# Loading the last 64 tokens of q and k with groups of tokens outermost instead of heads

## The chip, the core and the metric

One core of a Trainium2 chip runs the whole program. The metric is the device time of one execution in microseconds; the time of the kernel before is the median of three runs. A profile of one execution lies beside it.

## What is computed

Windowed attention over 8 batches, 8 heads, 576 tokens and 64 dimensions, followed by a dense two-layer block over all 4608 tokens. The first four heads see the last 32 tokens ("plain"), the other four every fourth of the last 128 ("dilated").

```python
scores = scale * np.matmul(q, k.transpose(0, 1, 3, 2))
mask_plain = (rel >= 0) & (rel < window)                                             # window = 32
mask_dil = (rel >= 0) & (rel < window * dilation) & (rel % dilation == 0)            # dilation = 4
...
attn = softmax(np.where(masks, scores, -1e9))
x = np.matmul(attn, v).transpose(0, 2, 1, 3).reshape(B * S, H * D)
h = x @ w_in                   # 512 -> 2048
g = np.maximum(0.01 * h, h)
out = g @ w_out                # 2048 -> 512
```

## The kernel before

All work is put into a plan first: each task has its engines, a duration by a cost model, the tasks that it depends on and a priority. The planner lists the tasks in a fixed order, and the program issues them so; on the chip each engine then works through its own instructions in that order and waits on semaphores. Nearly all DMAs are issued by SyncE (SP), so their order is fixed too. The change alters no task, no duration in the model and no priority, so each engine's instructions stand in the same order in both kernels.

The batches are worked in order. The first two (those below `EARLY`) are treated otherwise than the later six: their q, k and v are loaded in rows of 256 elements, four tokens of 64 dimensions, so that tokens with the same remainder by four end up together. 576 tokens are 144 such groups, and a tile has 128 partitions. So each early batch comes in two parts: part 0 has the first 128 groups, part 1 the remaining 16 groups, which are the last 64 tokens. Part 1 is loaded for all eight heads at once by `load_rest` (line 519): one load of q and one of k into a staging tile `stg` of 128 partitions, one partition for each pair of head and group, 256 elements of q and 256 of k in each; a load of v follows. GpSimd casts the staged rows to fp16 into the tile `rest` (by the helper at line 344, which records every cast).

In `turn` (line 654), with `part == 1`, TensorE turns `rest` in eight transposes (line 719) into the PSUM tile `tpb`. There the partitions are the 64 dimensions (twice), and the columns are numbered by o (0 for q, 1 for k), by the token's place in its group, and by the partition that the row had in `rest`. VectorE then copies (helper `move`, recorded at line 640) the columns of each head into the tiles `qbd` and `kt`, which the profile calls `slots`, at the places where the scores' matmuls want them. Where the slots of two heads' pairs are neighbours, one copy moves both; here that is so for every copy, 64 partitions by 128 elements each, eight copies for each early batch, in the order q, k for one half of the partitions and q, k for the other, the dilated heads ahead of the plain ones. Their order of columns differs: q of the dilated heads is written in runs of 16, k of the dilated heads to every fourth column; q of the plain heads in runs of 16, and k of the plain heads in runs of four tokens, read with a step of 128 columns.

Around this part in the program stand the casts of the weights w_in and w_out (line 344, on GpSimd, VectorE and, at line 342, ScalarE), the first dense layer (`up`, line 1069, with its activation at line 1080), the second (`down`, line 1240), the scores (lines 862 to 881) and the values of part 0 and 1 (lines 913 to 945), the normalisation (lines 957 to 963). In the first 60 us SP issues the q, k and v of the two early batches and all weights; the loads of `load_rest` are issued at 13.09 and 13.93 us for the first batch and at 41.26 and 45.06 us for the second, in the order of the plan's `FIRST`.

Of the kernel before, what the change touches and what calls it, by code (L numbers as in the profile page):

```python
# [211 lines left out]
def kernel(  # L212
# [14 lines left out]
    B, H, S, D = q.shape  # L227
# [7 lines left out]
    HS = S * D  # L235
# [16 lines left out]
    def bank(name, dt=FP32):  # L252
        return ps.tile([128, 512 if dt == FP32 else 1024], dt, name=name)

    def at(tl, p0, p1, off, *dims):

        row = tl.ap[0][0]
        return bass.AP(tensor=tl.tensor, offset=tl.offset + p0 * row + off,
                       ap=[[row, p1 - p0]] + [list(d) for d in dims])

    def dram(t, off, *dims):
        return bass.AP(tensor=t.tensor, offset=t.offset + off, ap=[list(d) for d in dims])
# [6 lines left out]
    PAD = 32  # L269
# [39 lines left out]
    tpb = bank("tp", FP16)  # L309
# [42 lines left out]
    def ring(name, n, users):  # L352

        r = rings.setdefault(name, [])
        waits = r[-n] if len(r) >= n else []
        r.append(users)
        return (len(r) - 1) % n, waits
# [24 lines left out]
    def clear_ones(slots, deps, prio=-700):  # L382
        for i in slots:
# [10 lines left out]
                   lambda e, h=h: ENG[e].memset(sides[64 * h:64 * h + 64, 64 * h:64 * h + 64], 1.0),  # L394
# [124 lines left out]
    def load_rest(b, prio):  # L519


        _, r_old = ring("REST", 1, r_users := [])
        sn, s_old = ring("STG", NST, s_users := [])
        st, lo = stg[sn], []
        for o, src in ((0, q), (1, k)):
            lo.append(load("SP", at(st, 0, 128, o * 256, [1, 256]),
                           dram(src, b * H * HS + 512 * D, [HS, 8], [4 * D, 16], [1, 256]),
                           128, 1024, s_old, prio))
        c = cast(at(rest, 0, 128, 0, [128, 8], [D, 2], [1, D]),
                 at(st, 0, 128, 0, [D, 8], [0, 2], [1, D]), 1024, lo + r_old, prio)  # L530
        s_users.append(c)
        vs, v_old, v_users = v_late[b]
        spread = bass.AP(tensor=vs.tensor, offset=vs.offset + 1024,
                         ap=[[4 * vs.ap[0][0], 16], [256, 4], [1, 256]])
        lv = load("SP", spread,
                  dram(v, (b * H + 4) * HS + 512 * D, [4 * D, 16], [HS, 4], [1, 256]),
                  64, 1024, v_old + [t_vr], prio)
        for vi in (2, 3, 0, 1):
            vt, d_users = kept[b, vi]
            c_v = []  # L540
            if vi >= 2:
                c_v = [cast(at(vt, 0, 64, 0, [1024, 2], [128, 4], [1, D]),
                            at(vs, 0, 64, 1024 + (vi - 2) * 256, [512, 2], [D, 4], [1, D]), 512,
                            [lv] + d_users, prio + 30)]
                v_users += c_v
            visits[b, vi, 1] = rest, [c], r_users, vt, c_v + seen_ones[b, vi], d_users
# [107 lines left out]
    def turn(b, hp, part, prio):  # L654
# [11 lines left out]
        if b >= EARLY:  # L666
            if tn not in s_clear:
                f = slots.bitcast(FP32)
                s_clear[tn] = [add((("POOL", 0.36), ("DVE", 0.34)), None, 0.2, old,
                                   lambda e, h=h: ENG[e].memset(  # L670
                                       at(f, 64 * h, 64 * h + 64, tn * S + 32 * (1 - h), [64, 9], [1, 32]),
                                       0.0), prio, 0.0, "set") for h in range(2)]
            qs = kb[:, PAD:PAD + S]
            for h in range(2):
                p0 = 64 * h
# [69 lines left out]
        if part == 1:  # L745
            if hp == 2:
                _, q_old = ring("TP", 1, q_users := [])
                tq = add("PE", 0.46, 0.25, c_qk + [t_id] + q_old, turn_in(tpb, na, 0, 8), prio, 0.2)
                n_users.append(tq)
                turned_rest[b] = tq, q_users  # L750
            tq, q_users = turned_rest[b]
            other = slot_of[b, hp ^ 1]
            two = 2 if abs(other[0] - tn) == 1 else 1
            if two == 2 and hp % 2:
                new = pair_moves[b, hp ^ 1]
            else:
                new, busy = [], users + other[1] * (two == 2)
                for hh in range(2):
                    h, p0 = 4 * (hp // 2) + hp % 2 + 2 * hh, 64 * hh
                    for o, bk in ((0, qb), (1, kb)):  # L760
                        x, dims = 512 * o + 16 * h, [[128, 4], [1, 16]]
                        if dil:
                            c, to = (0, [[144, 4], [4, 16]]) if o else (hh * S + 128, [[144, 4], [1, 16]])
                        elif o:
                            c, to, dims = PAD + 512, [[4, 16], [1, 4]], [[1, 16], [128, 4]]
                        else:
                            c, to = hh * S + 488, [[24, 4], [1, 16]]
                        step = PAD + S if o else 2 * S
                        new.append(move(at(bk, p0, p0 + 64, c, [step, two], *to),
                                        at(tpb, p0, p0 + 64, x, [16, two], *dims), 64 * two,  # L770
                                        [tq] + zq + zk + (busy if dil and o else []), prio))
                pair_moves[b, hp] = new
            q_users += new
            ev += new
        else:
            if b == 0 and not dil:
                if hp == 0:
                    _, q_old = ring("TP", 1, q_users := [])
                    both = []
                    for x in range(2):  # L780
                        n_x, c_x, u_x = visits[b, x, 0][:3]
                        both.append(add("PE", 0.23, 0.25, c_x[:1] + [t_id] + q_old,
                                        turn_in(tpb[:, 512 * x:512 * x + 512], n_x, 0), prio, 0.2))
                        u_x.append(both[-1])
                    two_q.append((both, q_users))
                tq, q_users = two_q[0]
                x = 512 * hp
                made = q_to((x, x), 0, 96, tq)
                q_users += made
            else:  # L790
                _, q_old = ring("TP", 1, q_users := [])
                tq = add("PE", 0.23, 0.25, c_qk[:1] + [t_id] + q_old, turn_in(tpb, na, 0), prio, 0.2)
                n_users.append(tq)
                for lo, hi in ((0, 128),) if dil else ((0, 120), (120, 128)):
                    q_users += q_to((lo, lo), lo, hi, [tq])
                made = q_users[:]
            if b == 0:
                _, k_old = ring("TPK", 1, k_users := [])
                kb_in, c_in, k_eng = tpk, 0, ("DVE", "ACT")
            else:  # L800
                k_old, k_users, kb_in, c_in, k_eng = q_old, [], tpb[:, 512:1024], 512, ("DVE",)
            if (b, hp) == (0, 1):
                k_eng = ("DVE",)
            tk = add("PE", 0.23, 0.25, [c_qk[1], t_id] + k_old, turn_in(kb_in, na, 512), prio, 0.2)
            n_users.append(tk)
            k_users += k_to(tpk if b == 0 else tpb, c_in, 0, 128, 0, 128,
                            [tk] if b == 0 else [tk, tq], k_eng)
            if b == 0:
                k_turned.extend(k_users)
            else:  # L810
                for t in q_users:
                    t.deps.append(tk)
                q_users += k_users
            ev += k_users if b else made + k_users
            if b:
                ev += q_users
            if b == 0 and hp == 1:
                later = []
                for hh in range(2):
                    p0 = 64 * hh  # L820
                    for i, n, c in ((96, 24, 384), (120, 8, 480)):
                        later.append(move(
                            at(qbd[tn - 1], p0, p0 + 64, hh * S + c, [2 * S, 2], [24, 4], [1, n]),
                            at(tpb, p0, p0 + 64, i, [512, 2], [128, 4], [1, n]), 8 * n,
                            tq + zq + t_zero[tn - 1][0], prio + 30))
                q_users += later
                for x in range(2):
                    t_x, u_x, e_x = (tn, users, ev) if x else slot_of[b, 0]
                    slot_of[b, x] = t_x, u_x, e_x + later
                return ev, users, qb, kb  # L830
# [734 lines left out]
    for t, u in zip(pe, pe[1:]):  # L1565
        if t.start > WARM:
            break
        x = t.start + t.dur + 0.1
# [45 lines left out]
```

## Time and profile before

| what | value |
|---|---|
| median of 3 runs | 307.77 us (305.67 to 308.3) |
| the profiled execution | 304.43 us, its span 302.6 us |
| granted TensorE clock | 0.994 in the mean |
| busy: PE, DVE, ACT, POOL | 290.3, 248.3, 214.2, 129.4 us |
| DMA | 47.64 MB, 157302 packets, mean 157 GB/s |
| copies of line 640 | 45, of which 16 are those of part 1 (64x128 elements) |

PE is TensorE's matmuls, PEld its weight loads, DVE VectorE, ACT ScalarE, POOL GpSimd, SP SyncE. "Busy" is time in which an engine has an instruction under way, without waiting. The chain that ended last is followed back from the last instruction, at each step to what released it. The DMA share is the mean over the core's 16 DMA engines; it can be a little over 1 since packets overlap. Lines like `POOL rest L344 <- DMA stg<-in_k_dram: 0.8, 2, 0.5` say who waited for whom: us in total, how often, the longest.

### The profile page before, as it was taken

Reading aid. Unit: us, or ns where it says so; the run is one execution under the profiler, and the core shown is the slowest. Engines: PE = TensorE matmul, PEld = TensorE weight load, DVE = VectorE, ACT = ScalarE, POOL = GpSimd, SP = SyncE. Lnnn points to the kernel's source line nnn. Section 1 sums busy time; section 2 is a strip of 40 time slices with the busy share of each in tenths; the row PEclk is TensorE's granted clock in tenths of the full one; section 3 lists DMA queues with packets and bytes.
Section 4 is the critical chain, followed back from the end, with each engine's and each line's share of the span. In section 5 each row is a group of like instructions: output and inputs, shape, how many; then the busy total and the mean of one; then the engine's idle time right before and its main releaser. Section 6 shows DMA issues by size and latency. Waiting matters only on the chain.

```text
span 302.6 us, 8081 instructions
## 1 busy us (share of the span) xinstructions
PE 290.3 (96%) x3027; PEld 230.2 (76%) x3027; DVE 248.3 (82%) x485; ACT 214.2 (71%) x523; POOL 129.4 (43%) x175
## 2 busy tenths in 40 slices
PE   5989979999999999999999999999999999999995
PEld 2635644657997788778877787778999999999984
DVE  5778897675999999998997997989998868577662
ACT  3799773696896885885867787466868877777511
POOL 5378776159828828835926656761000000000000
PEclk9999989999999999999999999999999999999999
DMA  7999998979889879658985988973102210031034
GB/s 247 334 339 404 397 363 174 185 149 209 157 173 199 147 152 218 121 131 146 189 156 137 165 173 167 162 191 101 42 2 77 64 37 1 2 107 35 2 111 132
DMA packets 157302, 47.64 MB, mean 157 GB/s; under 512 B 137296, under 2 KB 154576, under 8 KB 157264
## 3 DMA queue, kind: packets, MB, share of 16 engines
q1 hardware_dynamic: 156688, 46.79, 65.2%
q8 instruction: 23, 0.38, 0.5%
q10 hardware_dynamic: 576, 0.35, 0.4%
q14 instruction: 15, 0.12, 0.1%
HBM read 37.68 MB, written 9.44 MB: 156 GB/s over the span
## 4 chain that ended last, share of the span: by engine, by line
PE 62%; DVE 11%; ACT 7%; POOL 6%; DMA 5%; SPq 5%; issue 3%; POOLq 0%; ACTq 0%; DVEq 0%
PE fps L1331 16%; PE hps L1069 12%; PE hps L1153 7%; PE tp L1331 6%; SPq L333 5%; PE fps L1240 4%; PE ops L1153 3%; DMA stg<-in_q_dram 3%; PE ops L1012 2%; ACT gt L1080 2%; DVE ee L1022 2%; ACT w_in L342 2%; DVE turned L693 2%; PE sps L1153 2%; POOL slots L699 2%
## 5 line engine op out<-in xcount | busy, mean ns | idle before, releaser
L1069 PE MATMUL hps<-xt,w_in 128*128 128x384 f16 (+1 forms) x556 | 99.5, 307 | 0.8 <-DVE w_in L344 0.4
L1080 ACT ACTIVATE gt<-hps 128x384 f16<-128x384 f32 (+1 forms) x139 | 63.4, 460 | 26.2 <-PE hps L1069 25.1
L1331 PEld LDWEIGHTS <-gt 128*128 128x128 f16 x768 | 72.9, 98 | 9.6
L1069 PEld LDWEIGHTS <-w_in 128*128 128x128 f16 x576 | 49.1, 98 | 22.7 <-issue 1.2
L344 POOL CAST v_all<-vst 64x1152 f16<-64x1152 f32 (+3 forms) x36 | 41.1, 1150 | 15.6 <-DMA vst<-in_v_dram 14.1
L1331 PE MATMUL fps<-w_out,gt 128*128 128x256 f16 x368 | 47.5, 272 | 0.0
L344 POOL CAST nat<-stg 128x576 f16<-128x576 f32 (+1 forms) x49 | 34.5, 726 | 16.9 <-DMA stg<-in_q_dram 10.6
L1041 DVE TENSOR_TENSOR xt<-ops,rc 128x288 f16<-128x288 f32 x48 | 26.7, 557 | 5.3 <-PE ops L1012 2.6
L1022 DVE TENSOR_TENSOR ee<-ee,late_m 128x384 f16<-128x384 f16 (+1 forms) x48 | 25.4, 540 | 2.9 <-ACT ee L1019 2.8
L678 DVE STREAM_TRANSPOSE slots<-nat 64x64 f16<-64x64 f16 (+1 forms) x48 | 23.9, 497 | 0.5
L699 POOL COPY slots<-turned 64x512 f16<-64x512 f16 x24 | 19.0, 791 | 8.5 <-DVE turned L693 7.7
L1153 PEld LDWEIGHTS <-w_in 128*128 128x128 f16 x256 | 22.1, 98 | 0.5
L1033 ACT ACTIVATE rc<-rc 128x288 f32<-128x288 f32 x48 | 21.3, 449 | 0.5
L1360 ACT COPY stg<-fps 128x512 f32<-128x512 f32 (+1 forms) x24 | 12.8, 535 | 12.2 <-PE fps L1331 10.7
L693 DVE STREAM_TRANSPOSE turned<-nat 128x576 f16<-128x576 f16 (+1 forms) x24 | 17.6, 738 | 2.1 <-POOL nat L344 1.2
L706 POOL COPY slots<-turned 128x576 f16<-128x576 f16 x12 | 9.8, 819 | 20.7 <-DVE turned L693 20.4
L1240 PE MATMUL fps<-w_out,gt 128*128 128x512 f16 x64 | 16.9, 400 | 0.0
L1012 PEld LDWEIGHTS <-sides 128*128 128x128 f16 x240 | 14.0, 97 | 3.7 <-issue 0.8
L1153 PEld LDWEIGHTS <-stg 128*128 128x128 f16 x192 | 16.5, 98 | 0.3
L1163 ACT COPY rc<-hps 128x384 f32<-128x384 f32 x24 | 11.5, 479 | 7.4 <-PE hps L1153 5.5
L640 DVE COPY slots<-tp 64x128 f16<-64x128 f16 (+7 forms) x43 | 13.8, 334 | 3.5 <-PE tp L719 2.7
L1012 PE MATMUL ops<-ee,v_all 128*128 128x96 f16 (+2 forms) x240 | 16.4, 199 | 0.0
(145 smaller groups left out, 597.5 us busy)
## 6 DMA issues: line engine op xcount, KB each, us to landing
stg<-in_q_dram SPq DMA_DIRECT2D x48, 144.0 KB, 3.4
stg<-in_k_dram SPq DMA_DIRECT2D x48, 144.0 KB, 2.9
vst<-in_v_dram SPq DMA_DIRECT2D x12, 288.0 KB, 3.6
vst<-in_v_dram SPq DMA_DIRECT2D x24, 128.0 KB, 2.7
gt<-in_moe_w_in_dram SPq DMA_DIRECT2D x5, 512.0 KB, 7.8
xt<-in_moe_w_out_dram SPq DMA_DIRECT2D x3, 512.0 KB, 10.2
gt<-in_moe_w_out_dram SPq DMA_DIRECT2D x3, 512.0 KB, 9.5
vst<-in_v_dram SPq DMA_DIRECT2D x3, 384.0 KB, 10.2
```

The lines of the kernel that those rows point to most:

```text
L344: ENG[e].tensor_copy(out=dst, in_=src)
L678: nc.vector.transpose(at(qb, p0, p0 + 64, p0 + c, *dims), na[p0:p0 + 64, S + c // 2:S + c // 2 + n])
L693: lambda e, xb=xb, o=o, n=n: nc.vector.transpose(xb[:, 0:n], na[:, o * S:o * S + n]),
L699: lambda e, xb=xb, p0=64 * h: ENG[e].tensor_copy(out=at(qb, p0, p0 + 64, p0, [128, 4], [512, 2], [1, 64]), in_=at(xb, p0, p0 + 64, 0, [1, ...
L1012: nc.tensor.matmul(at(bk, 0, 128, o, *dims), stationary(s), et[:, c:c + n], start=i == 0, stop=i == len(parts) - 1, skip_group_check=True)
L1022: lambda e: nc.vector.tensor_tensor(out=et[:, 0:w], in0=et[:, 0:w], in1=mk, op=ALU.mult), prio + 0.1)
L1041: lambda e: nc.vector.tensor_tensor(out=dst, in0=at(ot, 0, 128, 0, *src), in1=at(rt, 0, 128, 0, *src), op=ALU.mult), prio + 0.2)
L1069: nc.tensor.matmul(ht[:, 0:n], at(w_in, 0, 128, i * DFF + j // 2 * 256 + j % 2, [2, 128]), at(xt[m % 2], 0, 128, i * 1152 + x0 + x, [1, n] ...
L1080: lambda e: nc.scalar.activation(out=gt[c % NG][:, j * n_c + x:j * n_c + x + n], in_=ht[:, 0:n], func=AF.Prelu, alpha=0.01),
L1153: nc.tensor.matmul(bk[:, 192 * jj:192 * jj + 192], w(i, 2 * jp + jj), x(i), start=first and jj == 0 and i == 0, stop=jj == 1 and i == 1, s ...
L1240: nc.tensor.matmul(ft, g[:, j * n_c + tt * 128:j * n_c + tt * 128 + 128], w_out[:, j * DM:j * DM + DM], start=(j == 0), stop=(j == NJ - 1))
L1331: nc.tensor.matmul(bk[:, x:x + HN], tl[:, off + j * step:off + j * step + 128], rhs(j), start=first and x == 0 and j == 0, stop=j == HJ - ...
```

## The change

In `load_rest` the two outer dimensions of the source are exchanged: 16 groups of tokens (step 4 x 64 elements) come first, then the 8 heads (step 576 x 64 elements). The destination is the same 128 partitions by 256 elements, so that partition p holds head p mod 8 and group p div 8, where before it held head p div 16 and group p mod 16. In `turn` the copies follow: the columns of one head start at h instead of 16 h, and lie eight apart instead of side by side; the two heads of one copy are 1 apart instead of 16.

```diff
         for o, src in ((0, q), (1, k)):
             lo.append(load("SP", at(st, 0, 128, o * 256, [1, 256]),
-                           dram(src, b * H * HS + 512 * D, [HS, 8], [4 * D, 16], [1, 256]),
+                           dram(src, b * H * HS + 512 * D, [4 * D, 16], [HS, 8], [1, 256]),
                            128, 1024, s_old, prio))
...
                     for o, bk in ((0, qb), (1, kb)):
-                        x, dims = 512 * o + 16 * h, [[128, 4], [1, 16]]
+                        x, dims = 512 * o + h, [[128, 4], [8, 16]]
                         if dil:
                             c, to = (0, [[144, 4], [4, 16]]) if o else (hh * S + 128, [[144, 4], [1, 16]])
                         elif o:
-                            c, to, dims = PAD + 512, [[4, 16], [1, 4]], [[1, 16], [128, 4]]
+                            c, to, dims = PAD + 512, [[4, 16], [1, 4]], [[8, 16], [128, 4]]
                         else:
                             c, to = hh * S + 488, [[24, 4], [1, 16]]
                         step = PAD + S if o else 2 * S
                         new.append(move(at(bk, p0, p0 + 64, c, [step, two], *to),
-                                        at(tpb, p0, p0 + 64, x, [16, two], *dims), 64 * two,
+                                        at(tpb, p0, p0 + 64, x, [1, two], *dims), 64 * two,
                                         [tq] + zq + zk + (busy if dil and o else []), prio))
```

The cast to `rest`, the transposes and the load of v are the same in both.

## The prediction

> **What bounds the kernel now.** I read the totals of the page first, then the stretches, the chain that ended last, the DMA issues, and at last the single instructions that the change touches. The totals and the granted clock:
>
> ```profile
> PE 290.3 (96%) x3027; PEld 230.2 (76%) x3027; DVE 248.3 (82%) x485; ACT 214.2 (71%) x523; POOL 129.4 (43%) x175
> ...
> PEclk9999989999999999999999999999999999999999
> ...
> PE 62%; DVE 11%; ACT 7%; POOL 6%; DMA 5%; SPq 5%; issue 3%; POOLq 0%; ACTq 0%; DVEq 0%
> ```
>
> The first line says that TensorE is busy nearly all the time, the last that it is 62% of the chain that ended last. The change touches only the first 56 us, so the question is what sets the pace there. The busy time by stretches (columns: us, PE, PEld, DVE, ACT, POOL, granted clock, DMA share, GB/s):
>
> ```profile
> 0.00:20.00 20.00, 15.47 (x129) 8.87 (x130) 13.06 (x41) 12.92 (x32) 10.00 (x25) 1.00 0.95 299
> 20.00:44.00 24.00, 20.76 (x183) 12.63 (x183) 20.78 (x56) 20.39 (x46) 19.77 (x32) 0.98 1.05 393
> 44.00:60.00 16.00, 16.00 (x125) 8.35 (x122) 11.96 (x29) 7.55 (x22) 7.02 (x10) 0.93 0.93 181
> ```
>
> From 20 to 44 us the DMA engines are full (share 1.05, 393 GB/s) and every engine is some 85% busy; from 44 us on TensorE has no idle time. So a delay of a load before 44 us can matter, and one behind it must reach TensorE to count. In the chain from 16 to 30 us stand ScalarE's casts of w_in and its activations, then TensorE's matmuls, from 37.7 to 42.5 us ScalarE, the normalisation and the `slots` copies on VectorE, then TensorE; the loads of `load_rest` and the cast to `rest` are nowhere in it. In the stretches of 4 us the granted clock is 0.87 from 40 to 44 and 0.70 from 44 to 48: a window of about 3.4 us at half speed, right behind the stretch in which TensorE was busy for 2.64 of 4 us. It costs 1.7 us. That is the largest single thing near the change.
>
> **The change, part by part.** *The loads.* For two batches `load_rest` issues one load of q and one of k (128 KB each) with 8 heads outermost; the change puts 16 groups of tokens outermost. Bytes, runs of 1 KB, issues and their order stay. What the old form does is seen in the DMA issues (size, then median us from issue to landing):
>
> ```profile
> vst<-in_v_dram SPq DMA_DIRECT2D x24, 128.0 KB, 2.7
> ...
> stg<-in_q_dram SPq DMA_DIRECT2D x2, 128.0 KB
> stg<-in_k_dram SPq DMA_DIRECT2D x2, 128.0 KB
> ...
> vst<-in_v_dram SPq DMA_DIRECT2D x2, 64.0 KB, 7.0
> ```
>
> A time to landing is given where each of the 16 DMA engines left its mark on the semaphore. Only the four loads of the change have none: the trace holds 28 marks fewer than 16 for each DMA, seven for each of them, which fits eight engines that carry the data and one mark for the eight that do not. The load of v beside them, whose outer count is 16 already, has all its marks. So I take it that the change spreads each load over 16 engines instead of 8. [...]
>
> The worth: at 393 GB/s over 16 engines 128 KB take 0.33 us, over 8 of them 0.67; a pair on 8 engines keeps these 0.67 us longer than needed. That is -0.67 us for each batch at the very most, -1.3 in all, if the loads behind set the pace; 0 if nobody waits. Who waits:
>
> ```profile
> POOL rest L344 <- DMA stg<-in_k_dram: 0.8, 2, 0.5
> ...
> PE hps L1069 <- DVE w_in L344: 0.4, 1, 0.4
> ...
> DVE w_in L344 <- DMA gt<-in_moe_w_in_dram: 0.4, 1, 0.4
> ```
>
> GpSimd's cast to `rest` waits 0.35 us in the first batch (21.65) and 0.49 in the second (48.57). In the first, GpSimd then casts v and w_in without a pause to 25.5 us, so 0.35 us can be passed to w_in; in the second the cast ends at 49.6 and its user, the eight transposes at line 719, comes at 53.4, so nothing is passed on. Of the loads behind, a w_in load makes VectorE wait 0.36 us at 23.2, and TensorE waits 0.43 us for a cast of VectorE at 28.8, but ScalarE, which stands in the chain from 16 to 30 us, waits there for no DMA. I take -0.2 us, nearer to the end of 0 because no DMA stands in the chain between 16 and 59 us. SP's issues behind the pair (w_in loads in the first batch; v, the late mask and batch 2 in the second) keep their order; the long issue at 41.26 (3.75 us) I read as a wait for room behind the 384 KB of v ahead of it, not for the pair.
>
> *The copies.* Sixteen copies of 64x128 elements (line 640) read the transposed tile in PSUM, eight a batch, two for q and two for k in each pair of heads. Single ones, in order q, k of the dilated heads, and k of the plain heads (ns):
>
> ```profile
> L640 DVE COPY slots<-tp x1: 215/215/215, 24.6 to 24.6; 64x128 f16<-64x128 f16 x1
> L640 DVE COPY slots<-tp x1: 438/438/438, 25.0 to 25.0; 64x128 f16<-64x128 f16 x1
> L640 DVE COPY slots<-tp x2: 216/244/271, 27.4 to 27.5; 64x128 f16<-64x128 f16 x2
> L640 DVE COPY slots<-tp x1: 283/283/283, 28.7 to 28.7; 64x128 f16<-64x128 f16 x1
> ```
>
> The q copies read and write runs of 16 neighbours: 215 ns. The plain k copies read every 128th element and write neighbours: 271 to 283. The dilated k copies read neighbours and write every fourth: 438. After the change a q copy reads every eighth element and writes neighbours; its nearest row is the plain k copy, so +60 ns, times eight, 0.48 us of VectorE in all, 0.24 a batch. A plain k copy reads every 128th element before and after, so 0. A dilated k copy already pays for its write; a strided read beside it is shown by no row. Bounds for that and for q: nothing at one end, +222 ns (438 less 216) at the other, for 12 copies 2.7 us. I take 0 for k. [...]
>
> On the path: in the first batch the copies stand between casts of w_in on VectorE (24.6 to 29.5), where TensorE waits 0.43 us for one such cast; of the 0.24 us I charge 0.1, since ScalarE's backlog there hides the rest (without that cover 0.24). VectorE's next idle moment is 0.54 us at 31.6, which ends the delay. In the second the eight copies (53.87 to 55.96) have their first user at 56.12, line 865, held by TensorE itself; the four dilated ones that it needs are done at 55.03, so 1.1 us cover the 0.12 added. Cost 0.
>
> *Sum.* -0.2 + 0.1 = -0.1 us on the profiled execution of 304.43 us (span 302.6 and 1.8 around it), so 304.3. The three runs shown lie higher: their median is 307.77, their mean 307.25. Less 0.1 that is 307.1 to 307.7; I say 307.4. The runs scatter by 2.6 us, so about 1% (3 us) is what a measurement of this kernel tells from no change.
>
> **The rivals.**
>
> *Faster: the front of the kernel is paced by DMA after all.* For it: GpSimd's casts follow the landings from 25 to 49 us (waits of 0.17, 0.25, 0.72, 0.54, 0.59, 2.11 and 0.49 us on DMA), and each engine fills its queue in program order. Then both 0.67 us come through, and if TensorE's stretch of 40 to 44 us closes up enough, the window at half clock goes too: -1.3 - 1.7 = -3.0, with the waits left over about -3.2: 304.5. Against it: the chain at 37.7 to 42.5 us is made of ScalarE, VectorE and TensorE. Chance 0.23.
>
> *Slower: the strided read holds VectorE, and TensorE falls idle into another window of half clock.* The place is 24.6 to 31 us, where the copies stand among the w_in casts. The price: up to 6 x 222 ns = 1.3 us of VectorE in the first batch, which its 0.54 us of idle time does not take up, so 0.8 us of idle TensorE, and a window like that at 43 us, 1.7 us, twice where the idle stretch straddles two: 0.8 + 3.4 = +4.2, 312.0; with one window +2.5. It passes 1% only with the second window or with a delay over 1.3 us. For it: TensorE is busy 3.35 of 4 us from 28 to 32 and 3.29 from 36 to 40, close to where the clock fell. Against it: PSUM reads with a far longer stride cost 60 ns. Chance 0.18.
>
> *The loads stay on eight engines.* Then only the copies' +0.1 is left, 307.9. The missing marks with an outer count of 8 and the full ones with 16 speak against it. Chance 0.04.
>
> **How the numbers follow.** No change that can be measured: 0.55 for my sum and 0.04 for loads that stay on eight engines, 0.59 within 1%. Faster by more 0.23, slower by more 0.18; both are larger than the sum alone suggests, because windows of half clock come in steps of 1.7 us and a program of fixed order shifts as a whole. The likeliest alone would be 305.6 to 309.0. The range reaches to the faster case and past one extra window: 303.9 to 310.2; left out are most of the slower rival and little on the other side.
>
> **What would show it.** In the profile after, the two 128 KB lines should carry a time to landing. GpSimd's wait for `stg<-in_k_dram` should fall below 0.8 us. The q copies should last about 275 ns, the dilated k copies 438, the plain ones 271 to 283; the sixteen together 0.5 us more. The window at half clock should still lie near 43 us. The prediction is wrong if copies of 64x128 take 450 ns or more, if the chain between 16 and 59 us has a DMA in it, or if windows of half clock come or go.

## The result

The changed kernel is slower: 309.57 us (median of 12 runs, 307.72 to 312.26) against 306.69 us for the kernel before on the same chip (12 runs, 304.47 to 310.95). The ratio is 1.0115, with a 95% interval of 1.0084 to 1.0147, some 3.5 us. The ratio leaves out the executions in a slower state, so it is not the quotient of the two medians (1.0094). The forecast was 307.4 us and no change that can be measured. The time lies in the range that was given, but by luck: the range reaches so far up for one more window of half clock, and none came. The case is the slower one, by none of the rivals' mechanisms.

The profiled execution of the changed kernel has a span of 308.7 us, 6.1 more than the one before. That overstates the difference, since the execution profiled before was faster than the fastest of its 12 runs here. The totals, the clock and the chain that ended last, from the page of the changed kernel:

```profile
PE 289.2 (94%) x3027; PEld 229.5 (74%) x3027; DVE 249.8 (81%) x485; ACT 214.6 (70%) x523; POOL 127.8 (41%) x175
...
PEclk9999999999999999999999999999999999999999
...
PE 56%; DMA 13%; DVE 12%; SPq 8%; POOL 5%; ACT 3%; issue 2%; POOLq 0%; ACTq 0%; DVEq 0%
```

No engine has much more work (TensorE 1.1 us less, VectorE 1.5 more), and the clock is full throughout. The window at half clock near 43 us, 1.7 us in the profile of before (a clock of 0.50 in each us from 43 to 46, 0.81 in the next), is not there in this execution; so a window of half clock isn't what was lost. What grew is the share of DMA in the chain, from 5 to 13%, and of SP's queue, from 5 to 8%. That points to a place and no more, since the chain differs between executions. In e3 below, which is the kernel before once more, it is

```profile
PE 74%; DVE 11%; ACT 4%; DMA 4%; SPq 3%; issue 3%; DVEq 0%; ACTq 0%
```

and e1 and e2 below have the same 9% of DMA and 8% of SP's queue, though e1 is as slow as the changed kernel and e2 as fast as the one before. Where TensorE lost time is seen in the busy time by stretches (columns: us, PE, PEld, DVE, ACT, POOL, granted clock, DMA share, GB/s). First the kernel before, in two stretches that the prediction did not look at:

```profile
100.00:160.00 60.00, 59.61 (x666) 46.80 (x665) 56.67 (x94) 43.55 (x108) 35.49 (x42) 1.00 0.81 155
160.00:200.00 40.00, 39.42 (x428) 30.54 (x425) 35.25 (x62) 28.41 (x70) 25.37 (x29) 1.00 0.85 166
```

The changed kernel:

```profile
20.00:44.00 24.00, 19.16 (x166) 11.60 (x165) 20.91 (x52) 19.60 (x43) 20.15 (x32) 1.00 1.05 395
44.00:60.00 16.00, 15.49 (x135) 8.66 (x135) 13.81 (x33) 7.77 (x23) 8.24 (x11) 1.00 0.89 173
...
100.00:160.00 60.00, 58.82 (x649) 45.96 (x648) 55.23 (x93) 43.01 (x105) 33.37 (x39) 1.00 0.81 153
160.00:200.00 40.00, 35.39 (x379) 26.74 (x377) 30.32 (x55) 26.18 (x63) 21.79 (x27) 1.00 0.80 156
```

From 20 to 60 us TensorE's busy time, multiplied by the granted clock, is 20.3 + 14.9 = 35.2 us before and 34.7 us after: 0.6 us lost. From 100 to 200 us it is busy 99.0 us before and 94.2 after: 4.8 us lost. Laid side by side, the starts of the same matmuls in the two traces say the same (start before, and how much later in the changed kernel, us):

| 24 | 34 | 44 | 64 | 105 | 145 | 155 | 175 | 195 | 296 |
|---|---|---|---|---|---|---|---|---|---|
| 1.30 | 1.98 | 1.52 | 0.44 | 0.44 | 0.40 | 1.40 | 3.60 | 6.08 | 6.08 |

The front ends 0.44 us late, nothing is lost up to 145 us, and the rest is lost by 195. That is some 100 us behind the last instruction that the change touched, in loads, casts and matmuls that are the same in both kernels, and the DMA engines move less there (156 GB/s instead of 166 from 160 to 200 us). Who waits, in the waits of before and then of after (us in total, times, longest):

```profile
POOL v_all L344 <- DMA vst<-in_v_dram: 14.1, 9, 4.4
...
POOL nat L344 <- DMA stg<-in_q_dram: 10.6, 5, 4.1
...
POOL nat L344 <- DMA stg<-in_k_dram: 5.8, 3, 3.3
...
DVE slots L712 <- POOL nat L344: 1.2, 1, 1.2
...
DVE turned L693 <- POOL nat L344: 1.2, 1, 1.2
```

```profile
POOL v_all L344 <- DMA vst<-in_v_dram: 19.5, 10, 4.3
POOL nat L344 <- DMA stg<-in_q_dram: 18.6, 8, 4.7
...
POOL nat L344 <- DMA stg<-in_k_dram: 13.6, 5, 8.2
...
DVE slots L712 <- POOL nat L344: 5.3, 3, 2.1
DVE turned L693 <- POOL nat L344: 4.7, 2, 3.6
...
POOL rest L344 <- DMA stg<-in_k_dram: 0.2, 1, 0.2
```

GpSimd's casts of q, k and v wait 51.7 us for DMA instead of 30.5, the first two batches included; behind 60 us, where only the six later batches are left, it is 38.3 instead of 20.0. VectorE waits 10.0 us for the casts to `nat` instead of 2.4. Only the last line belongs to the changed loads, and it got better (0.8 before).

That the load queue has little slack there could have been read before the change. A piece of the chain of before, in order of time (start, us, what):

```profile
160.94 0.42 SPq L333
...
163.41 0.61 SPq L333
...
166.07 4.33 DMA stg<-in_q_dram
...
170.51 0.85 POOL nat L344
```

At 159 us the chain leaves TensorE, and goes on by SP's queue, a 144 KB load and the cast behind it. In the changed kernel it comes to SP's queue at 131 us already, goes back to TensorE at 150.6, and leaves it again at 164.9; some of the pieces:

```profile
137.98 2.49 DMA vst<-in_v_dram
...
144.12 4.36 DMA stg<-in_q_dram
...
166.90 2.21 DMA vst<-in_v_dram
...
172.13 3.12 DMA stg<-in_q_dram
```

Against that the changed loads did what the diff says. Their lines among the DMA issues now carry a time to landing, and the program has 157334 packets instead of 157302, eight more for each of the four:

```profile
stg<-in_q_dram SPq DMA_DIRECT2D x2, 128.0 KB, 8.1
stg<-in_k_dram SPq DMA_DIRECT2D x2, 128.0 KB, 5.6
```

The 32 packets are of 4 bytes: the trace of the changed kernel has 5137 of that size, that of before 5105, while the marks on the semaphores go from 5108 to 5136. So an old load has nine marks where a new one has 16, and eight packets of 4 bytes fewer. What leaves the ninth mark no trace shows.

The copies of the first batch in the changed kernel, by windows that hold one, two or three of them (count, ns min/median/max, first and last start):

```profile
L640 DVE COPY slots<-tp x2: 273/351/429, 26.4 to 26.6; 64x128 f16<-64x128 f16 x2
L640 DVE COPY slots<-tp x2: 294/368/441, 27.0 to 27.2; 64x128 f16<-64x128 f16 x2
L640 DVE COPY slots<-tp x3: 272/284/294, 29.3 to 29.8; 64x128 f16<-64x128 f16 x3
L640 DVE COPY slots<-tp x1: 282/282/282, 30.6 to 30.6; 64x128 f16<-64x128 f16 x1
```

The four q copies take 273, 294, 284 and 294 ns instead of 215, 228, 216 and 227; dilated k 429 and 441 instead of 438 and 439; plain k 272 and 282 instead of 271 and 283.

### The profile page after: what moved, and what is told of

It reads as the page before. It is cut to its first block, busy times and chain, and to the rows that moved or that the text cites. A ratio compares the mean times of both kernels' runs of the same rounds, so it can differ in the third digit from the quotient of the medians.

```text
span 308.7 us, 8081 instructions
## 1 busy us (share of the span) xinstructions
PE 289.2 (94%) x3027; PEld 229.5 (74%) x3027; DVE 249.8 (81%) x485; ACT 214.6 (70%) x523; POOL 127.8 (41%) x175
## 2 busy tenths in 40 slices
DMA packets 157334, 47.64 MB, mean 154 GB/s; under 512 B 137328, under 2 KB 154608, under 8 KB 157296
## 3 DMA queue, kind: packets, MB, share of 16 engines
q1 hardware_dynamic: 156720, 46.79, 63.8%
## 4 chain that ended last, share of the span: by engine, by line
PE 56%; DMA 13%; DVE 12%; SPq 8%; POOL 5%; ACT 3%; issue 2%; POOLq 0%; ACTq 0%; DVEq 0%
PE fps L1331 16%; PE hps L1069 11%; SPq L333 8%; PE hps L1153 7%; DMA stg<-in_q_dram 6%; PE tp L1331 5%; PE fps L1240 4%; PE ops L1153 3%; DMA wst<-in_moe_w_in_dram 3%; DMA vst<-in_v_dram 2%; DMA stg<-in_k_dram 2%; PE ops L1012 2%; POOL nat L344 2%; PE sps L1153 2%; DVE ee L1022 2%
## 5 line engine op out<-in xcount | busy, mean ns | idle before, releaser
L344 POOL CAST v_all<-vst 64x1152 f16<-64x1152 f32 (+3 forms) x36 | 39.3, 1101 | 20.4 <-DMA vst<-in_v_dram 19.5
L1022 DVE TENSOR_TENSOR ee<-ee,late_m 128x384 f16<-128x384 f16 (+1 forms) x48 | 26.7, 569 | 2.7 <-ACT ee L1019 2.6
L699 POOL COPY slots<-turned 64x512 f16<-64x512 f16 x24 | 17.9, 745 | 3.3 <-DVE turned L693 2.2
L1006 PEld LDWEIGHTS <-slots 128*128 128x128 f16 x240 | 12.8, 97 | 7.6 <-POOL slots L699 3.4
L1012 PEld LDWEIGHTS <-v_all 128*128 128x128 f16 x240 | 14.7, 98 | 3.9 <-issue 1.8
L1019 ACT ACTIVATE ee<-sps 128x384 f16<-128x384 f32 (+1 forms) x24 | 12.2, 509 | 7.5 <-PE sps L1006 7.4
```

The lines of the kernel that those rows point to most:

```text
L344: ENG[e].tensor_copy(out=dst, in_=src)
L699: lambda e, xb=xb, p0=64 * h: ENG[e].tensor_copy(out=at(qb, p0, p0 + 64, p0, [128, 4], [512, 2], [1, 64]), in_=at(xb, p0, p0 + 64, 0, [1, ...
L1012: nc.tensor.matmul(at(bk, 0, 128, o, *dims), stationary(s), et[:, c:c + n], start=i == 0, stop=i == len(parts) - 1, skip_group_check=True)
L1022: lambda e: nc.vector.tensor_tensor(out=et[:, 0:w], in0=et[:, 0:w], in1=mk, op=ALU.mult), prio + 0.1)
```

## The experiments

Two figures are given for each run besides its time. *Stream* is the time that SP takes from issuing the first 144 KB load of batch 2 (at 46.6 to 51.8 us) over the next 148 issues; those instructions are the same in all kernels here. *PE 100–200* is TensorE's busy time in that stretch. *Lead* is worked out from the access patterns: how many descriptors (entries of an engine's queue: one for each row or run that it moves, and one for its mark) some engines have been given more than the others once the early batches are loaded. No trace names the engines; the marks that are missing in each trace agree with the number of engines given here, and so do the packets: e15 has 157862, 528 more than the changed kernel, which makes 256 runs and eight marks for each of its two loads, and e18 157598, 264 more, 128 runs and four marks for each. That all loads on eight engines take the same eight is the author's assumption. Each old 128 KB load gives eight engines 16 rows and a mark, so 17; four of them give 68. (e9's only profile is of an execution that took 725.17 us, for a reason that is not known, so it has no entries.) Ratios are over 6 to 12 runs of each kernel and 12 to 29 of the kernel before; stream and PE 100–200 come from one execution each. Between before and e3, the same kernel, stream differs by 0.9 us; between e2 and e3, which run alike, PE 100–200 differs by 2.9.

| kernel | lead, on engines | ratio to before | 95% interval | stream, us | PE 100–200, us |
|---|---|---|---|---|---|
| before | 68 on 8 | 1 | | 114.5 | 99.03 |
| e3 before again | 68 on 8 | 1.0005 | 0.9977 to 1.0032 | 115.4 | 99.63 |
| e2 copies only | 68 on 8 | 0.9999 | 0.9975 to 1.0022 | 115.4 | 96.77 |
| e17 | 134 on 8 | 1.0016 | 0.999 to 1.0042 | 113.7 | 99.61 |
| e15 | 66 on 8 | 0.9989 | 0.996 to 1.0019 | 113.2 | 97.42 |
| e18 | 66 on 4 | 1.0031 | 1.0002 to 1.006 | 116.3 | 96.67 |
| e5 | 34 on 8 | 1.002 | 0.9984 to 1.0056 | 115.8 | 99.36 |
| e6 | 34 on 8 | 0.9996 | 0.9968 to 1.0025 | 115.0 | 96.73 |
| e7 | 34 on 8 | 1.006 | 1.0028 to 1.0093 | 115.1 | 96.27 |
| e13 | 33 on 8 | 1.0054 | 1.002 to 1.0088 | 116.2 | 96.34 |
| e12 | 17 on 8 | 1.0059 | 1.0029 to 1.0089 | 117.1 | 95.56 |
| e9 | 4 on 8 | 1.0097 | 1.0062 to 1.0132 | – | – |
| e11 | 4 on 2 | 1.0134 | 1.0094 to 1.0174 | 117.4 | 94.41 |
| after | 0 | 1.0115 | 1.0084 to 1.0147 | 118.3 | 94.20 |
| e1 loads only | 0 | 1.0113 | 1.0075 to 1.0151 | 120.0 | 94.71 |
| e4 after again | 0 | 1.0113 | 1.0071 to 1.0156 | 117.8 | 94.46 |
| e8 | 0 | 1.0122 | 1.008 to 1.0165 | 116.5 | 95.86 |
| e10 | 0 | 1.0116 | 1.0074 to 1.0159 | 117.3 | 94.43 |
| e14 | 0 | 1.0112 | 1.008 to 1.0144 | 117.9 | 94.13 |
| e16 | 68 on 8, and 33 on 4, 33 on 2 | 1.0101 | 1.0063 to 1.014 | 113.2 | 99.63 |

The profiles behind this table also show that the program ends at a nearly fixed time after the stream. From the last of those issues to the end of the span it is 140.8 to 142.9 us in all of them, while the spans go from 302.6 to 310.0 us. So a kernel can lose by a late begin of the stream or by its length. And SP has no spare time in the stream: the pauses between its instructions add up to 9.7 us in each profile, so all that differs is how long the issues last, with what they wait for. The 72 of them that load 144 KB take 57.0 us before and 63.8 us after; they take 55.1 to 60.5 us in the profiles with a lead of 33 or more, and 60.5 to 63.8 in the others.

### Which half of the change

e1 has the new loads and reads them with the old copies, e2 the old loads with the new copies, so that in both the columns of other heads and tokens are taken for the last 64 tokens of the early batches, with as many instructions of the same sizes. e3 and e4 are the kernels before and after once more.

The edit of e1 against the changed kernel:

```diff
-                        x, dims = 512 * o + h, [[128, 4], [8, 16]]
+                        x, dims = 512 * o + 16 * h, [[128, 4], [1, 16]]
...
-                            c, to, dims = PAD + 512, [[4, 16], [1, 4]], [[8, 16], [128, 4]]
+                            c, to, dims = PAD + 512, [[4, 16], [1, 4]], [[1, 16], [128, 4]]
...
-                                        at(tpb, p0, p0 + 64, x, [1, two], *dims), 64 * two,
+                                        at(tpb, p0, p0 + 64, x, [16, two], *dims), 64 * two,
```

And of e2 against it:

```diff
-                           dram(src, b * H * HS + 512 * D, [4 * D, 16], [HS, 8], [1, 256]),
+                           dram(src, b * H * HS + 512 * D, [HS, 8], [4 * D, 16], [1, 256]),
```

> The loads of load_rest have groups of tokens outermost, as in the changed kernel; the sixteen copies read the columns of the kernel before (so the last 64 tokens of the first two batches land under wrong heads and places). Spread theory (the four loads on 16 DMA engines instead of 8 disturb the queue of loads behind them, and the changed kernel's 1.15% come from there): 1.008 to 1.015 of before. Copy theory (the 60 ns more of each q copy move the engines' fixed orders against each other): 0.995 to 1.004.

> The copies read every eighth column, as in the changed kernel; the loads keep heads outermost, on 8 DMA engines (so the last 64 tokens of the first two batches land under wrong heads and places). Spread theory: 0.996 to 1.004 of before, the q copies at 275 to 295 ns. Copy theory: 1.008 to 1.015.

> The kernel before once more, for a second profile of it. Both theories: ratio 1 within 0.4%. If the queue of loads sets the pace behind 47 us, the time of this profile and the time at which SP issues the first load of the third batch (46.95 us in the first profile) move together; if TensorE alone sets it, they do not.

> The changed kernel once more, for a second profile of it. Ratio to before 1.008 to 1.015. Spread theory: SP issues the first load of the third batch 1 to 2 us later than in the profiles of before. Copy theory: within 0.5 us of these.

e1 is 1.0113, e2 0.9999: the loads are the whole effect, the copies are free within 0.25%. e3 and e4 run as the kernels that they repeat (1.0005 and 1.0113). That the stream of the changed kernel begins 1 to 2 us later, as was expected for e4, did not hold: it begins at 47.57 us there, against 46.95 and 47.95 in the two profiles of the kernel before. In stretches, e1 first and then e2 (columns as above):

```profile
100.00:160.00 60.00, 58.02 (x641) 44.92 (x638) 54.61 (x89) 42.68 (x104) 33.69 (x39) 1.00 0.77 148
160.00:200.00 40.00, 36.70 (x390) 27.75 (x387) 31.63 (x59) 26.67 (x64) 20.54 (x26) 1.00 0.79 155
```

```profile
100.00:160.00 60.00, 59.65 (x662) 46.64 (x659) 57.04 (x94) 43.56 (x108) 34.46 (x41) 1.00 0.82 154
160.00:200.00 40.00, 37.11 (x396) 28.32 (x394) 32.38 (x58) 26.05 (x62) 23.08 (x28) 1.00 0.83 162
```

The DMA share is 0.82 and 0.83 with the old loads and 0.77 and 0.79 with the new ones. In the kernels before and after the difference is smaller: 0.81 in both from 100 to 160 us, 0.85 and 0.80 from 160 to 200.

### Which batch

In e5 only the first batch has the new loads, with the copies to match, in e6 only the second (`b == 1` in place of `b == 0`).

```diff
-                           dram(src, b * H * HS + 512 * D, [4 * D, 16], [HS, 8], [1, 256]),
+                           dram(src, b * H * HS + 512 * D,
+                                *(([4 * D, 16], [HS, 8]) if b == 0 else ([HS, 8], [4 * D, 16])), [1, 256]),
```

> Only the first batch has the new loads and copies, the second has heads outermost and its copies of before. Front theory (the lag arises where the new loads run, and each pair of loads on 16 engines pushes the queue behind it back): about half of the loss, 1.004 to 1.008 of before. Lasting theory (the even use of all 16 engines leaves the queue in a state in which the later batches' loads, unchanged themselves, are issued more slowly; any load on 8 engines ahead of them breaks it): 0.997 to 1.004, since the second batch still has two such loads.

> Only the second batch has the new loads and copies. Front theory: about half of the loss, 1.004 to 1.008 of before. Lasting theory: near before (0.997 to 1.004) if a load on 8 engines anywhere is enough, near the changed kernel (1.008 to 1.015) if it has to stand right ahead of the later batches' loads.

Neither half costs what the whole does (1.002 and 0.9996, both intervals below 1.006). A place where one of the loads collides with something would give the loss to one batch. So either pair of old loads is enough to keep the time, and what counts is something that it leaves behind. The old loads give eight engines more to do than the other eight; either that lead in descriptors or in bytes could last, or the time of an issue could count.

### A load beside the changed ones, on eight engines or on sixteen

All further kernels but e12, e16 and e17 are the changed kernel with one more load behind the pair of each early batch (in e13 and e14 of the first alone), into columns of `stg` that nobody reads. The load is issued within the task of the k load; only its call is shown. In e7 it is a copy of the old q load (128 KB, heads outermost, eight engines), in e8 one of the new form (sixteen).

```diff
+        nc.sync.dma_start(at(st, 0, 128, 512, [1, 256]),
+                          dram(q, b * H * HS + 512 * D, [HS, 8], [4 * D, 16], [1, 256]))   # e7
+                          dram(q, b * H * HS + 512 * D, [4 * D, 16], [HS, 8], [1, 256]))   # e8
```

> The changed kernel with one more load of 128 KB for each of the two batches, behind the load of k: q's rows once more, heads outermost, so on 8 engines, into unused columns of the staging tile. Nothing uses them. Front theory: 1 to 2 us more than the changed kernel (two more issues of 0.6 us and 0.67 us of eight engines each): 1.014 to 1.020 of before. Lasting theory: faster than the changed kernel although it moves more, 0.998 to 1.008 of before.

> As the run with one more load on 8 engines, but that load has groups of tokens outermost, so it goes over 16 engines. Front theory and lasting theory: both 1.012 to 1.018 of before, 0.5 to 1.5 us over the changed kernel (two more issues of 0.6 us, 0.33 us of all engines each).

256 KB more through eight engines bring the ratio to 1.006, the same through sixteen leave it at 1.0122; the intervals (up to 1.0093, from 1.008) just overlap. More bytes, in the busiest stretch for DMA, buy back about half.

### Fewer bytes: rows of 1 KB

The number of rows n is 8 in e9, 16 in e10 and 2 in e11.

```diff
+        nc.sync.dma_start(at(st, 0, n, 512, [1, 256]), dram(q, 512 * D, [HS, n], [1, 256]))
```

> The changed kernel with one more load of 8 rows of 1 KB for each of the two batches, which goes over 8 engines, one row on each; nothing uses it. If it matters only that the 16 engines have not been given the same number of descriptors: 0.998 to 1.004 of before, although two more issues of 0.4 us stand on SP. If the imbalance has to be large (each of the old loads gives eight engines 16 rows and a mark, the others nothing): 1.010 to 1.016.

> The same with 16 rows of 1 KB, which go over 16 engines, one row on each: the price of the extra issue alone. Both theories: 1.010 to 1.016 of before.

> The same with 2 rows of 1 KB, which go over 2 engines. If any difference between some engines is enough: 0.998 to 1.006 of before. If half of the engines have to differ from the other half: 1.009 to 1.016.

e10 is 1.0116, as the changed kernel: an issue more in each early batch costs nothing that can be measured. Eight rows on eight engines (e9, 1.0097) and two on two (e11, 1.0134) can't be told from it either. A load that merely uses eight engines isn't enough.

### One old load in four

> The changed kernel, but the load of q of the first batch, and its copies, as before: one load of the four on 8 engines. If one is enough: 0.997 to 1.004 of before. If the effect grows with the number of such loads (two of the four made the kernel as fast as before): 1.003 to 1.009.

In e12 only the q load of the first batch has its old form (the edit of e5 with `(b, o) != (0, 0)` as the condition). At 1.0059, with an interval of 1.0029 to 1.0089, it lies between the two kernels: a quarter of the old loads brings some half of the difference back.

### Many descriptors, few bytes

Each row is 32 runs of 64 B; eight such rows are 16 KB, an eighth of a changed load, but 33 descriptors with the mark for each engine. In e13 `ns` is `(8,)`, for the first batch only; in e14 `(16,)`, for the first only; in e15 `(8,)`, for both early batches. e16 is the kernel before, with `(4, 2)` for the first batch only.

```diff
+        for n in ns:
+            nc.sync.dma_start(at(st, 0, n, 512, [16, 32], [1, 16]), dram(q, 0, [HS, n], [D, 32], [1, 16]))
```

> The changed kernel with one more load in the first batch: 8 rows of 32 runs of 64 bytes, on 8 engines, so eight engines get 32 descriptors and a mark more than the others, as many as from two of the old 128 KB loads, but an eighth of a load's bytes. Nothing uses them. If the number of descriptors matters: 0.998 to 1.005 of before. If bytes or the time for which eight engines are held matter: 1.008 to 1.015.

> The same load over 16 engines (16 rows of 32 runs of 64 bytes): the price of the issue and of the short runs alone. Both theories: 1.009 to 1.016.

> The load of 8 rows of 32 runs of 64 bytes in both early batches: eight engines are 66 descriptors ahead, as in the kernel before with its 68. If the number of descriptors matters: 0.998 to 1.005 of before. If bytes or time matter: 1.008 to 1.016.

> The kernel before with two more loads of 32 runs of 64 bytes a row in the first batch, one of 4 rows on 4 engines and one of 2 rows on 2 engines, so that the engines stand at four different places instead of two. If engines at the same place are what costs: 0.990 to 0.998 of before. If two places are enough, or if it is bytes and time: 0.999 to 1.006.

e15 is the changed kernel with 32 KB more that nobody reads, and it runs as the kernel before: 0.9989, and the whole interval (to 1.0019) lies below that of the changed kernel. e13, half of it, is at 1.0054, between its two forecasts; e14, the same runs on sixteen engines, at 1.0112. Bytes don't decide, since e7 moved 256 KB for a lead of 34 and e15 32 KB for 66. Nor does the time for which eight engines are held: in the first 50 us a packet of 64 B takes 11.0 ns in the mean of e15, one of 1 KB 47.0 ns in the kernel before. By an estimate from these, e15's added loads hold each of eight engines for 0.7 us in all, the one old load of e12 for 0.75 and e7's added loads for 1.5, and of the three e15 alone is as fast as the kernel before. The lead in descriptors orders these runs, though not to the last: at leads of 33 and 34, e5 and e6 are at 1.002 and 0.9996, e7 and e13 at 1.006 and 1.0054, and the intervals of e6 and e7 do not meet. The waits of e15:

```profile
POOL v_all L344 <- DMA vst<-in_v_dram: 19.2, 9, 4.3
...
POOL nat L344 <- DMA stg<-in_k_dram: 10.3, 5, 4.8
POOL nat L344 <- DMA stg<-in_q_dram: 8.3, 3, 4.9
POOL slots L706 <- DMA stg<-in_q_dram: 7.0, 1, 7.0
...
DVE turned L693 <- POOL nat L344: 2.2, 1, 2.2
...
DVE slots L712 <- POOL nat L344: 1.9, 1, 1.9
```

GpSimd's casts wait 37.8 us for loads, against 51.7 in the changed kernel; one of its copies, which waits for no load in the changed kernel, waits 7.0 us here. VectorE waits 4.1 us for the casts, against 10.0.

e16 breaks the order of times, and neither of its forecasts held; its profile shows where. Its stream is the shortest, with e15's (113.2 us), and TensorE is busy 99.63 us from 100 to 200, but it lost more in the front than that gains. Its stretches from 20 to 60 us:

```profile
20.00:44.00 24.00, 19.01 (x143) 11.26 (x142) 15.40 (x42) 16.43 (x35) 15.71 (x25) 0.86 0.87 311
44.00:60.00 16.00, 13.94 (x128) 7.60 (x126) 14.28 (x37) 8.88 (x26) 10.29 (x14) 1.00 1.08 270
```

311 GB/s instead of 393 and a clock of 0.86 instead of 0.98 from 20 to 44 us: the casts of w_in on VectorE, GpSimd and ScalarE wait 6.6, 5.3 and 4.6 us for their loads into `gt`, TensorE's busy time multiplied by the clock is 30.3 us from 20 to 60 instead of 35.2, and the stream began at 51.8 us. (This is the fastest of its 12 runs, 307.58 us; their median is 309.93.) That the two loads on four and on two engines held them back is the obvious reading, but it wasn't tried by itself.

### Twice the lead, and half the engines

e17 is the kernel before with e15's loads, e18 the changed kernel with `ns = (4,)` in both early batches.

> The kernel before, with one more load in each early batch: 8 rows of 32 runs of 64 B on eight engines (16 KB, read by nobody). Eight engines are then 68 + 66 = 134 descriptors ahead of the other eight when the later batches start, twice what any kernel so far had. Theory 'the lead saturates': 68 are enough, the stream of loads of the later batches takes 113 to 115.5 us as in the runs with 66 and 68, and the time is 306 to 307 us, ratio 0.997 to 1.003. Theory 'the lead pays in proportion': the first 67 bought about 3.3 us, so another 66 buy as much again until TensorE no longer waits for the load queue; TensorE's share of 290 us leaves at most some 2 us: ratio 0.990 to 0.996. Theory 'the lead pays only near 68 (a position, not a lead)': 134 are as bad as 0, ratio 1.008 to 1.013, stream 116 us or more.

> The changed kernel, with one more load in each early batch on four engines only: 4 rows of 32 runs of 64 B (8 KB, read by nobody). Four engines are then 66 descriptors ahead of the other twelve. Theory 'what counts is how far some engines are ahead, whatever their number': as with eight engines 66 ahead, ratio 0.997 to 1.003 to the kernel before. Theory 'each engine that is ahead counts by itself': half the effect of eight engines, ratio 1.004 to 1.008. Theory 'two halves must be set apart, four engines do nothing': ratio 1.009 to 1.013, and the marks of the 16 engines of one 144 KB load spread 550 ns or more in the median as in the changed kernel.

e17 (1.0016, 0.999 to 1.0042) is the same as before: the lead neither pays on in the time nor is it a matter of one position near 68. SP's stream takes 113.7 us, hardly less than 114.5, and TensorE is 74% of the chain, as in e3. In the same profile the front was 2.8 us later (the stream began at 49.7 us instead of 46.9) and the clock 0.81 from 44 to 60 us; whether the longer queue in the front did that or chance, one profile can't tell.

e18 (1.0031, 1.0002 to 1.006) is above before and far below the changed kernel. That falls between two of the theories: four engines that lead do much of what eight do, and "four engines do nothing" is out: the marks of one 144 KB load spread 436 ns in the median there, not 550 or more. No kernel was measurably faster than the one before; e15 is the lowest ratio, and its interval holds 1.

## Why the prediction was wrong

The theory that stands: SP's stream of loads for the later batches sets the pace together with TensorE, and it runs some 3 us slower when all 16 DMA engines have been given equally many descriptors in the front than when some are well ahead. That the loads do it, and that uneven small loads undo it, the runs show (e1 and e2; e15 against e14); that the lead in descriptors is the measure, they make likely, with e5 to e7 as a scatter that it doesn't explain. Against the rivals "collision of a changed load", "bytes" and "time for which eight engines are held", "time of an issue" and "copies" stand e5 and e6, e15, e10, and e2. Point by point:

1. *What bounds the kernel.* "The change touches only the first 56 us, so the question is what sets the pace there" is the step that failed. So did "from 44 us on TensorE has no idle time", read as a shield for all that comes later. Up to 145 us that holds, and the load queue falls behind unseen; then its lag reaches TensorE. SP's 5% and the DMA's 5% of the chain stood on the page; the piece at 160 us shown above is part of them, and the prediction followed the chain only to 59 us.

2. *The loads spread over 16 engines.* Right: 32 packets more, and times to landing. The rival that they stay on eight is out. One reading on the way was wrong: the four loads are not the only ones without a time to landing. The line `vst<-in_v_dram SPq DMA_DIRECT2D x1, 352.0 KB` has none either, nor has any of the 120 DMAs that share the three semaphores of the four loads, where the trace counts 633, 626 and 633 marks instead of 640. The 28 missing marks, seven for each load, are right.

3. *The worth of that, −0.2 us, between −1.3 and 0.* Wrong in size and sign: e1 costs 1.13% of 306.7, or +3.5 us. Both bounds came from the time that a pair of loads occupies the engines ("−0.67 us for each batch at the very most"); that the same bytes in another split could slow the loads behind them was left out, with no row as a reason. The part in the front is too small to see: the stream begins at 48.60 us instead of 46.95 in the two profiles, but at 47.57 in e4 and 47.95 in e3. GpSimd's wait fell from 0.8 to 0.2 us as said, but it isn't a matter of the loads' form: e1, with the new loads, has 0.8 us too, and e3, with the old ones, none. That the q issue at 41.26 us (3.75 us) waits for room was the author's estimate; no trace names what it waits for, and the same issue takes 5.17 us in the changed kernel.

4. *The q copies, +60 ns each, dilated and plain k 0.* Right: +58 to +68, and within 10 ns. "0.24 us a batch" and the 0.1 charged for the first are not seen in e2 (0.9999, so between −0.8 and +0.7 us).

5. *Sum and case.* −0.1 us came of two terms, one right and one wrong by some 3.7 us.

6. *The slower rival* had the right sign and no more. Its mechanism, a strided read that leaves TensorE idle into windows of half clock, is refuted by e2 and by a clock at 1.00 in every stretch of the profile after. That windows of half clock come in steps of 1.7 us the executions bear out: their mean clocks lie near 1.00, 0.994, 0.989, 0.983 and 0.978, and 0.0055 of a span of 303 us is 1.7 us. That idle time of TensorE brings them no run shows: from 40 to 44 us it is busy 2.64 of 4 us before and 2.41 in the changed kernel, where the clock stays at 1.00. *The faster rival*, a front paced by DMA that gains from shorter loads, brought no gain: e1 is 1.13% slower.

7. *Signs to look for.* Two signs of being wrong came, and neither tells of this loss. The window at half clock near 43 us is gone in this profile; but it comes and goes with the execution, since e1, with the new loads, shows a clock of 0.91 from 44 to 60 us and e2, with the old ones, 1.00. And the chain of the changed kernel does have DMAs between 16 and 59 us, a load of w_in (9.41 us from 13.28 on) and one of q (7.01 us from 22.76 on); but e3, the kernel before once more, has such a load of w_in in its chain too (8.17 us from 12.86 on). So "no DMA stands in the chain between 16 and 59 us" was true of one execution, not of the kernel. The DMAs of the chain that cost the time lie behind 130 us.

What stays open is why a lead helps. The traces show what goes with it: the first and the last mark of one 144 KB load lie 370 to 468 ns apart in the median of the 96 such loads in each kernel with a lead of 34 or more, 510 in e13, and 528 to 600 with 17 or less, while a packet of 128 B takes as long as before (a mean of 13.0 ns before, 12.9 after). No run shows by what mechanism.

## What to carry to other kernels

When an edit changes a load, look at the whole chain for that queue, not only at the stretch around the edit: a queue that is just in time 100 us later is as exposed as the instruction next door. Spreading the loads over all engines was not free here (e1, 1.0113; the whole change, 1.0115), so for small loads beside a dense stream both forms are worth a run. And where halves of a change (e5, e6) cost nothing and the whole costs 1%, look for a state that adds up rather than for a place.

## What the runs showed of the hardware that was not expected

- Unequal work that was given to the DMA engines before 50 us acts on loads of the same program up to 160 us: 32 KB in 64 B runs, read by nobody, are worth 1.2% (e15, 0.9989, against the changed kernel, 1.0115), and the same kind of load on 16 engines nothing (e14, 1.0112).
- The effect goes with the number of descriptors rather than the bytes, and levels off: 0, 17 and 66 ahead on eight engines give 1.0115, 1.0059 and 0.9989, and four kernels with 33 or 34 lie between 0.9996 and 1.006; 134 give 1.0016, with a stream of 113.7 us where 66 gave 113.2.
- It is not free everywhere: the kernel before with two more loads on four and two engines (e16) had 311 GB/s instead of 393 in the stretch in which the front needs the weights.
